# Top-k attention and a low-rank mixer: the top-k mask of the first two batches made by ScalarE and GpSimd

## The chip, the cores and the metric

The kernel runs on one core of a Trainium2 chip, in one launch. The metric is device time in microseconds. The core's engines are TensorE (PE; its weight loads are PEld), VectorE (DVE), ScalarE (ACT), GpSimd (POOL) and SyncE (SP, which only issues transfers here); each works through its own instructions in order and waits for the others by semaphores.

## What is computed

Top-k attention over 8 batches, 8 heads, 576 positions, 64 features per head, and then a token-mixing and MLP block over 512 channels:

```python
scores = scale * np.matmul(q, k.transpose(0, 1, 3, 2))      # 576 x 576 for each head
kth = np.partition(scores, -32, axis=-1)[..., -32:-31]      # the 32nd largest of each row
scores = np.where(scores >= kth, scores, -1000000000.0)
scores = scores - np.max(scores, axis=-1, keepdims=True)
attn = np.exp(scores)
attn = attn / (np.sum(attn, axis=-1, keepdims=True) + 1e-09)
x = np.matmul(attn, v)                                      # heads side by side: (B, S, 512)

h = x.transpose(0, 2, 1) @ U @ V                            # low-rank mixing of positions
u = x + h.transpose(0, 2, 1)
out = u + np.maximum(u @ w_ch1, 0.0) @ w_ch2
```

Of each row of scores only the 32 largest get a weight; the other 544 must come out as zero.

## The kernel before

The heads are taken in pairs, 4 pairs to a batch, 32 in all. A pair has five steps: four row tiles of 128 rows, with one chunk of 576 scores for each of the two heads, and a fifth step in which the last 64 rows of both heads share one chunk. So there are 160 steps; step n belongs to pair g and tile t by `g, t = divmod(n, 5)`. The work of a step is written as a generator, `front`, whose parts the main loop calls one by one to place them among the work of other steps. The program's order on each engine is the order of these calls.

VectorE finds the threshold: `max` gives the eight largest of a row, `match_replace` strikes them out, and four rounds of this give the 32nd largest in `ms[c][:, 7:8]`. Then the mask is made in one of two ways: on VectorE, after the Exp, by one instruction that compares, multiplies and sums; or, for the second chunk of a two-chunk step, on GpSimd ahead of the Exp, by adding -3e38 to every score below the threshold.

```python
    def weigh(chunk, E, nmax, total=None):
        nc.scalar.activation(E, chunk, AF.Exp, bias=nmax, scale=SCALE, accum_out=total)

    def front(g, t):
        # ... chunks: the scores; Es: the tiles for the weights; sums: columns of den ...
        for c in order:
            ms[c] = first[:, c]
            nc.vector.max(ms[c], curs[c])
        yield
        pooled = n == 2 and (g, t) != (NPAIR - 1, NT - 1)
        for i in range(1, TOPK // 8):
            if i == 1:
                nc.scalar.mul(nmax[:, 0:n], first[:, 0:n, 0], -SCALE)
                for c in range(1 if pooled else n):
                    weigh(chunks[c], Es[c], nmax[:, c : c + 1])
            for c in order:
                nxt = attn.tile([P, S], F32, tag="rr", name="rr", bufs=3)
                nc.vector.match_replace(nxt, ms[c], curs[c], NEG)
                curs[c] = nxt
            for c in order:
                ms[c] = small.tile([P, 8], F32, tag="m8", name="m8", bufs=8)
                nc.vector.max(ms[c], curs[c])
            yield
        if pooled:
            nc.gpsimd.tensor_scalar(Es[1], chunks[1], ms[1][:, 7:8], NEG, ALU.is_lt, ALU.mult)
            nc.gpsimd.tensor_tensor(chunks[1], chunks[1], Es[1], ALU.add)
        for c in range(1 if pooled else n):
            nc.vector.scalar_tensor_tensor(out=Es[c], in0=chunks[c], scalar=ms[c][:, 7:8],
                in1=Es[c], op0=ALU.is_ge, op1=ALU.mult, accum_out=sums[c])
        yield
        if pooled:
            weigh(chunks[1], Es[1], nmax[:, 1:2], sums[1])
        yield
```

`scores` multiplies q and k into PSUM and has ScalarE copy the result to SBUF (`Ssb`). `turns` transposes the weights on TensorE and copies them back with ScalarE (`PT`), in three parts. `values` multiplies them with v into `O`, which ScalarE copies to `XT`. At the end of a pair VectorE makes the reciprocal of the sums, after it has added 1e-9:

```python
    def inverse(g, lo, hi):
        den = dens[g][:, lo:hi]
        nc.vector.tensor_scalar_add(den, den, 1e-9)
        nc.vector.reciprocal(den, den)
```

The MLP of a batch is `mlp`, a generator of single matmuls on TensorE. `fill` lets so many of them run at each place of the loop that the MLP of one batch is spread over the attention of the next. In the first batch there is no MLP to run yet. The weights come as 64-bit numbers; `next_params` has them turned into 32-bit ones by ScalarE, VectorE (a shift) and GpSimd (two additions), during the first six pairs or so. The loop for the first batch:

```python
        if n < ALONE:                       # ALONE = 20: the first batch
            next(turning, None)             # transposes of step n-2, the last two parts
            next(turning, None)
            scores(*divmod(n + 1, CH))      # scores of the next step
            fill()
            if n >= 1:
                turning = turns(*divmod(n - 1, CH))
            if n >= 2:
                values(*divmod(n - 2, CH))
            next(here)                      # first round of step n
            next_params(1)
            next(turning, None)             # transposes of step n-1, the first part
            fill()
            next(last, None)                # the Exp of step n-1 that comes after GpSimd's mask
            next(ready, None)
            next(here)                      # second round
            # ...
            next(here)                      # third round
            # ...
            next(here)                      # the masks
            fill()
            continue
```

Of the kernel before, what the change touches and what calls it, by code (L numbers as in the profile page):

```python
# [8 lines left out]
F32 = mybir.dt.float32  # L9
U8 = mybir.dt.uint8  # L10
U32 = mybir.dt.uint32
AF = mybir.ActivationFunctionType
ALU = mybir.AluOpType

TOPK = 32
NEG = -3.0e38


RESCALE = 2.0**-112

TINY = 0.4 * 2.0**-15

# [2 lines left out]
def kernel(  # L25
# [28 lines left out]
    nc = tc.nc  # L54
    B, H, S, D = q.shape
    P = 128
# [4 lines left out]
    NT, TAIL = 4, 64  # L61
# [3 lines left out]
    NPAIR = H // 2  # L65
# [7 lines left out]
    const = ctx.enter_context(tc.tile_pool(name="const", bufs=1))  # L73
    loads = ctx.enter_context(tc.tile_pool(name="loads", bufs=1))
    attn = ctx.enter_context(tc.tile_pool(name="attn", bufs=2))
    small = ctx.enter_context(tc.tile_pool(name="small", bufs=8))
# [34 lines left out]

    nudge = const.tile([P, 1], F32, name="nudge")
    nc.vector.memset(nudge, TINY)

    def rows(t):
        return P if t < NT else TAIL
# [148 lines left out]
    def scores(g, t):  # L265


        qkT = qkTs[g]
        n = rows(t)
        S2 = attn.tile([P, 2 * (S + TAIL)], F32, tag="Ssb", name="Ssb", bufs=3)  # L270
        scs = [ps_s.tile([P, 2, 512], F32, tag="sc", name="sc") for _ in range(2)]
        for i, sc in enumerate(scs):
            for h in range(2):
                nc.tensor.matmul(  # L274
                    sc[slice(0, n) if t < NT else half(h), h, 0:HALF],
                    lhsT=qkT[half(h), 0, cols(t)],
                    rhs=qkT[half(h), 1, i * HALF : (i + 1) * HALF],
                    start=True,
                    stop=True,
                )  # L280
        if t == NT:
            for i, sc in enumerate(scs):
                for h in range(2):
                    nc.scalar.copy(
                        S2[half(h), i * HALF : (i + 1) * HALF], sc[half(h), h, 0:HALF]
                    )
            S2s[g, t] = [S2[:, 0:S]]
            return

        main = S2.rearrange("p (h n) -> p h n", h=2)  # L290
        last = S2[:, MAIN : MAIN + 2 * TAIL].rearrange("p (h n) -> p h n", h=2)
        copy = nc.vector.tensor_copy if g + t == 0 else nc.scalar.copy
        copy(main[:, :, 0:HALF], scs[0][:, :, 0:HALF])  # L293
        nc.scalar.copy(main[:, :, HALF:MAIN], scs[1][:, :, 0 : MAIN - HALF])
        nc.scalar.copy(last, scs[1][:, :, MAIN - HALF : HALF])  # L295
        S2s[g, t] = [S2[:, 0:S], S2[:, S : 2 * S]]

    def weigh(chunk, E, nmax, total=None):

        nc.scalar.activation(E, chunk, AF.Exp, bias=nmax, scale=SCALE, accum_out=total)  # L300

    def front(g, t):

        if t == 0:
            dens[g] = small.tile([P, 2 * NT + 1], F32, tag="den", name="den", bufs=3)
        chunks, den = S2s.pop((g, t)), dens[g]
        n = len(chunks)
        E2 = attn.tile([P, 2 * S], F32, tag="E", name="E", bufs=3)  # L310
        Es = [E2[:, c * S : (c + 1) * S] for c in range(n)]
        sums = [den[:, 2 * t + c : 2 * t + c + 1] for c in range(n)]
        probs[g, t] = E2
        curs, ms = list(chunks), [None] * n
        first = small.tile([P, 2, 8], F32, tag="first", name="first", bufs=3)
        nmax = small.tile([P, 2], F32, tag="nmax", name="nmax", bufs=4)
        order = (1, 0) if n == 2 else (0,)
        for c in order:
            ms[c] = first[:, c]
            nc.vector.max(ms[c], curs[c])  # L320
        yield
        pooled = n == 2 and (g, t) != (NPAIR - 1, NT - 1)
        for i in range(1, TOPK // 8):
            if i == 1:
                nc.scalar.mul(nmax[:, 0:n], first[:, 0:n, 0], -SCALE)
                for c in range(1 if pooled else n):
                    weigh(chunks[c], Es[c], nmax[:, c : c + 1])
            for c in order:
                nxt = attn.tile([P, S], F32, tag="rr", name="rr", bufs=3)
                nc.vector.match_replace(nxt, ms[c], curs[c], NEG)  # L330
                curs[c] = nxt
            for c in order:
                ms[c] = small.tile([P, 8], F32, tag="m8", name="m8", bufs=8)
                nc.vector.max(ms[c], curs[c])  # L334
            yield
        if pooled:
            nc.gpsimd.tensor_scalar(Es[1], chunks[1], ms[1][:, 7:8], NEG, ALU.is_lt, ALU.mult)  # L337
            nc.gpsimd.tensor_tensor(chunks[1], chunks[1], Es[1], ALU.add)  # L338
        for c in range(1 if pooled else n):
            nc.vector.scalar_tensor_tensor(  # L340
                out=Es[c],
                in0=chunks[c],
                scalar=ms[c][:, 7:8],
                in1=Es[c],
                op0=ALU.is_ge,
                op1=ALU.mult,
                accum_out=sums[c],
            )
        if t == NT:
            del qkTs[g]  # L350
        yield
        if pooled:
            weigh(chunks[1], Es[1], nmax[:, 1:2], sums[1])
        yield

    def turns(g, t):
# [18 lines left out]

    def inverse(g, lo, hi):
        den = dens[g][:, lo:hi]
        nc.vector.tensor_scalar_add(den, den, 1e-9)
        nc.vector.reciprocal(den, den)

    def values(g, t):
# [155 lines left out]
    CH = NT + 1  # L537
# [27 lines left out]
    t = 0  # L565
# [3 lines left out]
    turning = ready = iter(())  # L569
    fronts = {}  # L570
    for n in range(STEPS + 2):
        g, t = divmod(n, CH)
        if n < STEPS:
            if t == 0 and g + 1 < NP:
                load(g + 1)
            if t == 1 and g + 1 < NP:
                ready = prep(g + 1)
            fronts[n] = front(g, t)
            next(fronts[n])
        here, last = fronts.get(n, iter(())), fronts.pop(n - 1, iter(()))  # L580
        if n >= ALONE - 1 and n <= ALONE:

            list(turning)
            if n < ALONE:
                scores(*divmod(n + 1, CH))
            list(turns(*divmod(n - 1, CH)))
            if n < ALONE:
                values(*divmod(n - 2, CH))
                next(here)
            values(*divmod(n - 1, CH))  # L590
            if n < ALONE:
                inverse(g, 0, 2 * NT)
                next(here)
                mixing.append(mixed(g, 1))
                fill()
                next(here)
                next(here)
                continue
            fill()
            scores(*divmod(n + 1, CH))  # L600
            next(here)
            while mixing:
# [3 lines that stand above are left out]
            next(last, None)  # L606
            next(here)
            fill()
            next(here)
            next(here)  # L610
            fill()
            continue
        if n < ALONE:
            next(turning, None)
            next(turning, None)
            scores(*divmod(n + 1, CH))
            fill()
            if n >= 1:
                turning = turns(*divmod(n - 1, CH))
            if n >= 2:  # L620
                values(*divmod(n - 2, CH))
            next(here)
            next_params(1)
            next(turning, None)
            fill()
            next(last, None)
            next(ready, None)
            next(here)
            fill()
            if n >= 2 and (n - 2) % CH == NT:  # L630
                mixing.append(mixed((n - 2) // CH, 3))
            next(here)
            if t == 1:
                next_params(1)
            next(here)
            fill()
            continue
        fill()
        next(turning, None)
        fill()  # L640
        next(turning, None)
        fill()
        next(ready, None)
        fill()
        if n - 2 >= ALONE:
            values(*divmod(n - 2, CH))
        if n + 1 < STEPS:
            scores(*divmod(n + 1, CH))
        next(here, None)
        next_params(1)  # L650
        if n - 2 >= ALONE and (n - 2) % CH == NT:
            mixing.append(mixed((n - 2) // CH, 4))
        fill()
        next(here, None)
        fill()
        if n <= STEPS:
            turning = turns(*divmod(n - 1, CH))
        next(turning, None)
        fill()
        next(here, None)  # L660
        next(last, None)
        if t in (1, 3):
            next_params(1)
        next(here, None)
        fill()
# [33 lines left out]
```

## Time and profile before

| | |
|---|---|
| median of 3 runs | 1859.95 us (1859.87 to 1863.38) |
| span of the profiled run | 1861.6 us |
| TensorE busy | 1750.6 us (94%) |
| VectorE busy | 1617.2 us (87%) |
| ScalarE busy | 1008.1 us (54%) |
| GpSimd busy | 635.7 us (34%) |
| mean granted TensorE clock | 0.966 |

The page also cuts the span into 40 slices and gives each a digit, the busy share in tenths:

```profile
PE   4565789999999999999999999999999999999999
DVE  7999999999999999999999999999999999996000
ACT  4666677555655555555555555555555555554111
POOL 4556466433333332323233332332323332322000
PEclk7677799999999999999999999999999999999999
```

Each digit stands for 46.5 us. TensorE's row and its clock are lower for the first five slices, which are the first batch; VectorE is nearly full from the second slice to the last batch, and then has nothing to do while TensorE runs the last MLP. An average over the whole span says little about a change that touches two batches of eight, so the times are read by stages below. In the groups of the trace a row has the line, the engine and the operation, the tiles written and read with their shapes, the count, the busy time in microseconds, the mean of one in nanoseconds, and behind the second bar the idle time just before, with what ended it.

### The profile page before, as it was taken

The numbers are of one execution on the slowest core, as the hardware profiler recorded it, in microseconds if no ns is written. First come the engines' busy times: TensorE is split into PE (matmuls) and PEld (weight loads), VectorE is DVE, ScalarE is ACT, GpSimd is POOL, SyncE is SP. The second block draws the span as 40 slices with busy tenths as digits, with TensorE's granted clock in tenths as the row PEclk, the third lists the DMA queues.
The fourth block names the chain that finished last, engine by engine and source line by source line (L and its number), as shares of the span: only waits on it lengthen the run. The fifth ranks groups of instructions, "written<-read, shape, count | busy, mean of one in ns | idle before, by whom it ended". The sixth has DMA issues, their size and how long they took to land.

```text
span 1861.6 us, 29241 instructions
## 1 busy us (share of the span) xinstructions
PE 1750.6 (94%) x10528; PEld 1324.0 (71%) x10528; DVE 1617.2 (87%) x3316; ACT 1008.1 (54%) x2466; POOL 635.7 (34%) x432
## 2 busy tenths in 40 slices
PE   4565789999999999999999999999999999999999
PEld 3443556787777877788777877788777877788677
DVE  7999999999999999999999999999999999996000
ACT  4666677555655555555555555555555555554111
POOL 4556466433333332323233332332323332322000
PEclk7677799999999999999999999999999999999999
DMA  3222222101000010110001010101001010000000
GB/s 98 76 72 75 63 81 81 28 23 32 15 21 22 23 29 21 30 25 24 23 13 31 21 32 20 28 22 27 14 24 27 25 30 21 10 8 7 6 14 12
DMA packets 127296, 58.23 MB, mean 31 GB/s; under 512 B 89904, under 2 KB 124976, under 8 KB 127152
## 3 DMA queue, kind: packets, MB, share of 16 engines
q1 hardware_dynamic: 126096, 56.10, 11.3%
q8 instruction: 84, 1.38, 0.3%
q14 instruction: 60, 0.49, 0.1%
q10 hardware_dynamic: 1056, 0.26, 0.1%
HBM read 46.89 MB, written 9.44 MB: 30 GB/s over the span
## 4 chain that ended last, share of the span: by engine, by line
PE 84%; DVE 10%; ACT 4%; issue 1%; POOL 1%; DMA 0%; POOLq 0%; SPq 0%; DVEq 0%; ACTq 0%
PE mm L472 27%; PE mm L491 26%; PE sc L274 9%; PE O L403 6%; PE tp L367 6%; DVE rr L330 4%; DVE m L334 3%; PE O L390 2%; PE up L447 2%; PE O L400 1%; DVE first L320 1%; PE tp L254 1%; PE tp L519 1%; PE up L449 1%; PE tp L372 1%
## 5 line engine op out<-in xcount | busy, mean ns | idle before, releaser
L334 DVE MAX8 m<-rr 128x8 f32<-128x576 f32 x864 | 614.8, 749 | 5.5
L491 PE MATMUL mm<-hT,w 128*128 128x256 f32 (+1 forms) x2048 | 562.2, 410 | 0.0
L472 PE MATMUL mm<-uT,w 128*128 128x256 f32 (+1 forms) x2048 | 557.9, 411 | 1.5 <-ACT hT L484 1.5
L337 POOL TENSOR_SCALAR E<-Ssb,m 128x576 f32<-128x576 f32 x127 | 285.2, 2246 | 650.7 <-DVE m L334 512.7
L472 PEld LDWEIGHTS mm<-uT,w 128*128 128x128 f32 x2048 | 363.3, 190 | 108.6 <-issue 27.6
L491 PEld LDWEIGHTS mm<-hT,w 128*128 128x128 f32 x2048 | 360.5, 190 | 97.7 <-issue 22.5
L330 DVE MATCH_REPLACE8 rr<-m,rr 128x576 f32<-128x576 f32 x576 | 427.8, 743 | 0.0
L367 PE MATMUL tp<-ident,E 128*128 128x128 f32 x1152 | 184.7, 285 | 53.8 <-ACT E L300 38.7
L368 ACT COPY PT<-tp 128x512 f32<-128x512 f32 x288 | 168.4, 585 | 114.9 <-PE tp L367 113.0
L300 ACT ACTIVATE E<-Ssb,nmax 128x576 f32<-128x576 f32 x288 | 223.8, 778 | 5.9 <-POOL Ssb L338 0.7
L367 PEld LDWEIGHTS tp<-ident,E 128*128 128x128 f32 x1152 | 144.9, 147 | 106.9 <-ACT E L300 50.7
L274 PE MATMUL sc<-qkT 64*128 64x288 f32 (+1 forms) x1280 | 212.5, 454 | 0.3 <-ACT Ssb L293 0.3
L330 DVE MATCH_REPLACE8 rr<-first,Ssb 128x576 f32<-128x576 f32 x288 | 211.8, 742 | 0.0
L320 DVE MAX8 first<-Ssb 128x8 f32<-128x576 f32 x288 | 205.4, 750 | 0.9 <-ACT Ssb L295 0.9
L340 DVE SCALAR_TENSOR_TENSOR E<-Ssb,m,E 128x576 f32<-128x576 f32 x161 | 137.8, 856 | 65.6 <-ACT E L300 48.2
L338 POOL TENSOR_TENSOR Ssb<-Ssb,E 128x576 f32<-128x576 f32 x127 | 178.9, 1408 | 10.6
L484 ACT ACTIVATE hT<-mm 128x320 f32<-128x320 f32 (+1 forms) x256 | 104.4, 408 | 119.8 <-PE mm L472 119.0
L412 ACT COPY XT<-O 128x128 f32<-128x128 f32 x128 | 34.0, 266 | 215.1 <-PE O L403 215.1
L403 PE MATMUL O<-PT,va 128*64 128x128 f32 x2048 | 147.7, 289 | 0.0
L274 PEld LDWEIGHTS sc<-qkT 64*128 64x128 f32 (+1 forms) x1280 | 110.2, 187 | 51.7 <-issue 25.4
L504 DVE TENSOR_TENSOR oT<-uT,mm 128x320 f32<-128x320 f32 (+1 forms) x8 | 3.6, 455 | 146.6 <-PE mm L491 146.6
L403 PEld LDWEIGHTS O<-PT,va 128*64 128x64 f32 x2048 | 116.0, 143 | 16.8 <-issue 2.9
(73 smaller groups left out, 1484.3 us busy)
## 6 DMA issues: line engine op xcount, KB each, us to landing
raw<-in_moe_w_ch_dram SPq DMA_DIRECT2D x32, 512.0 KB, 3.7
va<-in_v_dram SPq DMA_DIRECT2D x64, 128.0 KB, 2.5
out_dram<-ob SPq DMA_DIRECT2D x64, 128.0 KB, 1.9
ld_q<-in_q_dram SPq DMA_DIRECT2D x63, 128.0 KB, 2.8
ld_k<-in_k_dram SPq DMA_DIRECT2D x63, 128.0 KB, 2.8
ld_ends<-in_q_dram SPq DMA_DIRECT2D x32, 32.0 KB, 2.2
ld_ends<-in_k_dram SPq DMA_DIRECT2D x32, 32.0 KB, 2.2
vd<-in_v_dram SPq DMA_DIRECT2D x64, 16.0 KB, 2.0
```

Source lines behind the costliest of these rows:

```text
L274: nc.tensor.matmul(sc[slice(0, n) if t < NT else half(h), h, 0:HALF], lhsT=qkT[half(h), 0, cols(t)], rhs=qkT[half(h), 1, i * HALF : (i + 1 ...
L300: nc.scalar.activation(E, chunk, AF.Exp, bias=nmax, scale=SCALE, accum_out=total)
L320: nc.vector.max(ms[c], curs[c])
L330: nc.vector.match_replace(nxt, ms[c], curs[c], NEG)
L334: nc.vector.max(ms[c], curs[c])
L337: nc.gpsimd.tensor_scalar(Es[1], chunks[1], ms[1][:, 7:8], NEG, ALU.is_lt, ALU.mult)
L338: nc.gpsimd.tensor_tensor(chunks[1], chunks[1], Es[1], ALU.add)
L367: nc.tensor.transpose(tp[:, j, :], E2[:, a : a + P], ident)
L368: nc.scalar.copy(PT[:, NT * h : NT * h + NT], tp)
L403: nc.tensor.matmul(O[half(h)], lhsT=va[:, h, j, :], rhs=PT[:, NT * h + j], start=False, stop=(j == NT - 1),)
L472: nc.tensor.matmul(ph[:, 0:w], lhsT=w1[:, cc, f * P : (f + 1) * P], rhs=uT[:, cc, lo:hi], start=(cc == 0), stop=(cc == NC - 1),)
L491: nc.tensor.matmul(po[:, 0:w], lhsT=w2[:, f, c * P : (c + 1) * P], rhs=hTs[f][:, 0:w], start=(f == 0), stop=(f == NF - 1),)
```

## The change

It makes the mask in another way in the first two batches, to take work off VectorE. For all steps of the first eight pairs but the last two steps of the first batch ("eased" steps), both chunks go ahead of the Exp through ScalarE and GpSimd. ScalarE computes `Relu((threshold - score) * 2^96)`: zero for a score at or above the threshold, and a huge number, at least the smallest gap that two numbers can have times 2^96, for any other. GpSimd subtracts it from the score. The Exp then gives zero for every score that was struck out, and its own running sum is the denominator. VectorE keeps only the search for the threshold; the addition of 1e-9 goes to ScalarE. The two sections of the main loop are put in a new order to suit: the masks and Exps of a step are called during the next step, and all its transposes one step later.

```diff
+WIDEN = 2.0**96
...
+    eps = const.tile([P, 1], F32, name="eps")
+    nc.vector.memset(eps, 1e-9)
...
+    def eased(g, t):
+        return g < 2 * NPAIR and (g, t) not in ((NPAIR - 1, NT - 1), (NPAIR - 1, NT))
...
+        final = small.tile([P, 2, 8], F32, tag="final", name="final", bufs=4)
...
-        pooled = n == 2 and (g, t) != (NPAIR - 1, NT - 1)
-        for i in range(1, TOPK // 8):
+        ease = eased(g, t)
+        pooled = n == 2 and not ease and (g, t) != (NPAIR - 1, NT - 1)
+        early = range(0 if ease else 1 if pooled else n)
+        rounds = TOPK // 8
+        for i in range(1, rounds):
...
-                for c in range(1 if pooled else n):
+                for c in early:
                     weigh(chunks[c], Es[c], nmax[:, c : c + 1])
...
-                ms[c] = small.tile([P, 8], F32, tag="m8", name="m8", bufs=8)
+                ms[c] = final[:, c]
+                if i < rounds - 1:
+                    ms[c] = small.tile([P, 8], F32, tag="m8", name="m8", bufs=8)
...
-        for c in range(1 if pooled else n):
+        for c in early:
             nc.vector.scalar_tensor_tensor(
...
-        if pooled:
-            weigh(chunks[1], Es[1], nmax[:, 1:2], sums[1])
+        if ease:
+            least = small.tile([P, 2], F32, tag="least", name="least", bufs=3)
+            nc.scalar.mul(least[:, 0:n], final[:, 0:n, 7], WIDEN)
+            for c in order:
+                nc.scalar.activation(
+                    Es[c], chunks[c], AF.Relu, bias=least[:, c : c + 1], scale=-WIDEN
+                )
+                nc.gpsimd.tensor_tensor(chunks[c], chunks[c], Es[c], ALU.subtract)
+            yield
+        for c in order:
+            if c not in early:
+                weigh(chunks[c], Es[c], nmax[:, c : c + 1], sums[c])
+        if ease and t == NT:
+            nc.scalar.activation(den, den, AF.Identity, bias=eps)
         yield
...
-        nc.vector.tensor_scalar_add(den, den, 1e-9)
+        if not eased(g, NT):
+            nc.vector.tensor_scalar_add(den, den, 1e-9)
...
         if n < ALONE:
-            next(turning, None)
-            next(turning, None)
             scores(*divmod(n + 1, CH))
+            list(turning)
             fill()
-            if n >= 1:
-                turning = turns(*divmod(n - 1, CH))
             if n >= 2:
                 values(*divmod(n - 2, CH))
             next(here)
+            next(last, None)
             next_params(1)
-            next(turning, None)
             fill()
-            next(last, None)
             next(ready, None)
             next(here)
             fill()
+            next(last, None)
...
             next(here)
             fill()
+            if n >= 1:
+                turning = turns(*divmod(n - 1, CH))
             continue
         fill()
         next(turning, None)
+        if eased(*divmod(n - 2, CH)):
+            next(turning, None)
...
         next(here, None)
+        if eased(*divmod(n - 1, CH)):
+            next(last, None)
         next_params(1)
...
             turning = turns(*divmod(n - 1, CH))
-        next(turning, None)
+        if not eased(*divmod(n - 1, CH)):
+            next(turning, None)
```

## The prediction

> **What bounds the kernel now.** I read the stages first, because the change touches only the first two of eight batches. From the starts of the `first` rows on VectorE I took the stage borders: step 0 starts at 11.0 us, step 20 (the second batch) at 223.9, step 40 (the third) at 434.5; VectorE's last attention work ends at 1709. The busy time of each engine in these four stretches (columns: stretch, length, PE, PEld, DVE, ACT, POOL busy with counts, granted clock, DMA share, GB/s):
>
> ```profile
> 11.00:223.90 212.90, 129.57 (x747) 88.05 (x744) 206.49 (x431) 133.13 (x305) 111.99 (x80) 0.71 0.27 75
> 223.90:434.50 210.60, 201.37 (x1238) 148.76 (x1238) 204.99 (x425) 139.03 (x330) 106.46 (x70) 1.00 0.18 50
> 434.50:1709.00 1274.50, 1266.76 (x7871) 967.62 (x7870) 1200.57 (x2452) 710.80 (x1769) 411.84 (x263) 1.00 0.09 22
> 1709.00:1861.00 152.00, 147.24 (x660) 116.31 (x658) 3.64 (x8) 22.34 (x59) 3.21 (x4) 1.00 0.04 11
> ```
>
> The reader is to see three regimes. In the first batch VectorE is busy 97% and TensorE 61%: VectorE alone sets the pace. In the second, TensorE is at 96% and VectorE at 97%: two bounds within 4 us of each other. From the third on TensorE is at 99.4% and its work alone sets the end. So a microsecond gained before 434 us reaches the end whole, since what follows is a fixed sequence of TensorE work; but in the second batch only TensorE's idle time, 210.6 - 201.4 = 9.2 us, can be gained. Next the page's costliest groups, for the operations concerned:
>
> ```profile
> L334 DVE MAX8 m<-rr 128x8 f32<-128x576 f32 x864 | 614.8, 749 | 5.5
> ...
> L337 POOL TENSOR_SCALAR E<-Ssb,m 128x576 f32<-128x576 f32 x127 | 285.2, 2246 | 650.7 <-DVE m L334 512.7
> ...
> L300 ACT ACTIVATE E<-Ssb,nmax 128x576 f32<-128x576 f32 x288 | 223.8, 778 | 5.9 <-POOL Ssb L338 0.7
> ...
> L340 DVE SCALAR_TENSOR_TENSOR E<-Ssb,m,E 128x576 f32<-128x576 f32 x161 | 137.8, 856 | 65.6 <-ACT E L300 48.2
> L338 POOL TENSOR_TENSOR Ssb<-Ssb,E 128x576 f32<-128x576 f32 x127 | 178.9, 1408 | 10.6
> ```
>
> One mask costs VectorE 856 ns by its row; GpSimd does one in 2246 + 1408 ns. Last, VectorE's and GpSimd's rows around the denominator's addition (start, duration, engine, line):
>
> ```profile
> 73.02 1.41 DVE L320 MAX8 first<-Ssb 128x8 f32<-128x576 f32 x2
> ...
> 73.94 1.40 POOL L338 TENSOR_TENSOR Ssb<-Ssb,E 128x576 f32<-128x576 f32 x1
> 74.35 1.02 DVE L378 TENSOR_SCALAR den<-den 128x9 f32<-128x9 f32 x1
> 75.40 0.21 DVE L379 RECIPROCAL den<-den 128x9 f32<-128x9 f32 x1
> ```
>
> An addition on 9 columns takes 1.02 us. It ends at 75.37, when GpSimd's operation ends at 75.34; at 217.44 the same line, with GpSimd idle, took 0.15 us. It is a wait that the trace books as work.
>
> **What the Trainium skill says.** "Advanced Engine Details and Errata", VectorE Performance Modes, Mode Summary: VectorE's second memory port is shared with GpSimd, and instructions of the two-port mode and GpSimd's block each other. The pair above agrees (1.02 us against 0.15). "ScalarE: Activation LUTs", What ACT_TABLE_LOAD costs: an activation with a per-partition bias takes about 280 ns + 0.833 ns per column; by that a Relu on 576 columns is an estimated 760 ns. The trace's Exp of that form takes 778. The page's Table sets section says that relu comes in every set, so that no new table load is due; in this trace Exp, Relu, Sign and Copy run with one load in all. "TensorE: Matmul & The Clock Gate", What's actually happening, says that TensorE is granted half clock until it has been busy for some 3.4 us; the 0.71 of the first stretch agrees, and at 115.15 us, after 3.78 us idle, four transposes took 1.11 us, at 120.89 0.66.
>
> **The change part by part.** 38 of the first 40 steps change: 18 in the first batch (15 of two chunks, 3 of one), 20 in the second (16 and 4).
>
> *VectorE loses work.* One mask goes per step. From 114.18, where one starts, to 114.93, where the next operation starts, is 0.75 us; with 0.02 to 0.07 of gaps I take 0.77. The addition goes for seven pairs, at 1.05 with its gap. First batch: 18 x 0.77 + 3 x 1.05 = 17.0 us. Second: 20 x 0.77 + 4 x 1.05 = 19.6. Together 36.6 us, 1.97% of 1860: even if all of it reached the end, the 2% line would just be missed.
>
> *GpSimd loses a little.* It now takes 1.41 us for each chunk rather than 3.65 for one of two. First batch: 33 x 1.41 = 46.5 in place of 15 x 3.65 = 54.8. No bound. But a two-port operation of VectorE's, the weights' shift of 0.4 us, may now meet it at another time.
>
> *ScalarE gains work.* Each chunk gets a Relu. Neighbouring activations overlap (Exp at 121.42, next start 122.10), so 0.68 us net; each step gets a small scaling of the threshold (0.15 net) and one more accumulator read (0.1 net); a pair gets the small addition, 0.2. First batch: 33 x 0.68 + 18 x 0.25 + 3 x 0.2 = 27.5 us; second, with 36 chunks: 24.5 + 5 + 0.8 = 30.
>
> *Order moves.* A step's masks and Exp are now made during the next step, after VectorE's last maximum is long there, so that ScalarE shouldn't stall on it. The transposes of step n-2 all follow the scores of n+1, and the value products follow the transposes directly. No ring of tiles seems short: E, scores and denominators have three buffers, and the last reader of each is a step ahead of the next writer.
>
> *First batch in sum.* ScalarE: 133.1 + 27.5 = 160.6 us of work in what would be 213 - 17 = 196. Of its idle time before, some 80 us, the largest named waits are these (groups of ScalarE between 11 and 224 us, idle before and releaser at the end):
>
> ```profile
> L368 ACT COPY PT<-tp 128x512 f32<-128x512 f32 x35 | 20.2, 577 | 9.7 <-PE tp L367 9.6
> ...
> L412 ACT COPY XT<-O 128x128 f32<-128x128 f32 x16 | 4.2, 266 | 22.3 <-PE O L403 22.3
> L325 ACT ACTIVATE nmax<-first 128x2 f32<-128x2 f32 (+1 forms) x20 | 4.1, 206 | 11.6 <-DVE first L320 11.5
> ...
> L398 ACT ACTIVATE x<-O,den 64x64 f32<-64x64 f32 x6 | 1.9, 308 | 12.5 <-DVE den L379 12.5
> ```
>
> Waits on TensorE for transposes and value products, 32 us, cannot be hidden in the new order either: the products (0.79 + 1.61 us at half clock) start only after the last copy of the transposes, and ScalarE's next instruction in order is the copy of their result. With the mixing's 8 us that is 40. The waits on VectorE (12.5 + 11.6) shrink as ScalarE falls behind it. So ScalarE needs 160.6 + 40 to 52 = 201 to 213 us, against 196 on VectorE: the bound passes to ScalarE, and of 17 us some 0 to 12 stay. I take 8.
>
> *Second batch.* At most 9.2 us by TensorE. ScalarE goes from 139 to 169 of some 205, 82%; in its first half, with the weights still being converted, nearer 90%, and it evicts the hidden layer's PSUM there. I take 4.
>
> **Sum:** 1860 - 8 - 4 = 1848 us.
>
> **The rivals.** (a) *VectorE stays the bound in the first batch*: for it speaks the copying of scores a step ahead, so that ScalarE may lag; then 17 + about 7 = 24 us, 1836. (b) *ScalarE becomes the bound, fully*: its waits on TensorE add to the new work instead of shrinking, and the first batch takes as long as before or 5 us longer, with TensorE starved of evictions in the second: 1860 to 1868. For it speaks that the new order puts two round trips one after the other; against it that TensorE can now do the next scores early. (c) *Nothing carries over*: if the second batch's pace is TensorE's alone, the gain there is nil and only the first counts: 1850. The table (0.4% of idle TensorE after 434 us) speaks against a gain being given back later.
>
> **Range and chances.** The range runs from near (a) to a mild (b): 1833 to 1863. Over 2% faster needs 1822.8, below the ceiling of 1823.4: 0.02. Over 2% slower, 1897, needs a stall of 1 us or more in every changed step: 0.02. Within 2%: 0.96. Faster at all I hold for three in four.
>
> **What would show it.** The masks gone from VectorE's row: 161 to 123; 33 + 36 = 69 Relus near 760 ns; GpSimd's subtraction near 1408. Step 20 starting at about 216 rather than 223.9, and step 40 at about 422. ScalarE's busy share in the first batch near 78%, VectorE's falling from 97% to about 93%, idle before `first` and released by ScalarE's copies. In the third batch on the same pace, about 55 us for a pair. I'd be wrong if VectorE stayed at 97% in the first batch (rival a), if the subtraction or Relu took much longer side by side, if the denominator's reciprocal inherited the wait of 0.9 us, or if a new TensorE wait on E opened in the second batch.

## The result and the profile after

The changed kernel takes 1922.37 us, median of 4 runs (1921.31 to 1923.86), against 1859.91 for the one before: 1.0332 times as long, with a 95% interval of 1.0314 to 1.035. It lost 62 us where 12 were expected to be won.

First the same cut by stages as of the kernel before (stretch, length, PE, PEld, DVE, ACT, POOL busy, granted clock, DMA share, GB/s). The borders are again the starts of step 0, of step 20 (now 234.4) and of step 40 (now 485.8); at 527.5 step 43 starts, from which on the steps have their old lengths:

```profile
11.00:234.40 223.40, 141.13 (x749) 95.89 (x745) 198.41 (x392) 158.62 (x377) 101.66 (x83) 0.66 0.25 72
234.40:485.80 251.40, 211.41 (x1211) 152.63 (x1211) 190.98 (x382) 162.81 (x394) 90.99 (x70) 0.95 0.14 42
485.80:527.50 41.70, 36.22 (x221) 28.42 (x220) 32.91 (x68) 23.19 (x57) 18.70 (x13) 0.96 0.12 31
527.50:1768.00 1240.50, 1236.34 (x7682) 944.09 (x7681) 1166.85 (x2384) 695.05 (x1731) 399.52 (x255) 1.00 0.09 22
```

and of the kernel before the stretch that answers to the last one, from its step 43 on:

```profile
468.90:1709.00 1240.10, 1235.95 (x7679) 943.55 (x7678) 1167.49 (x2384) 695.07 (x1731) 400.14 (x256) 1.00 0.09 22
```

The first batch is 10.5 us longer (223.4 against 212.9), the second 40.8 us (251.4 against 210.6). No engine is full in the second batch any more: TensorE 84%, VectorE 76%, ScalarE 65%, GpSimd 36%. That is the picture of a chain of waits, not of an engine that has too much to do. From 527.5 us on nothing differs: 1240.5 us where the same steps took 1240.1.

The starts of single steps, from VectorE's rows, show where it happens (us):

| step | before | after | after - before |
|---|---|---|---|
| 10 (third pair) | 114.93 | 109.73 | -5.2 |
| 15 | 168.05 | 166.86 | -1.2 |
| 20 (second batch) | 223.94 | 234.43 | +10.5 |
| 30 | 331.84 | 360.04 | +28.2 |
| 40 (third batch) | 434.46 | 485.79 | +51.3 |
| 43 | 468.90 | 527.46 | +58.6 |

The gain is there at first: the first step of pair 1 (step 5) took 10.23 us where it had taken 11.21. It is lost again from the third pair on.

The page's groups that answer to those of before:

```profile
L376 POOL TENSOR_TENSOR Ssb<-Ssb,E 128x576 f32<-128x576 f32 x69 | 97.3, 1429 | 269.2 <-ACT E L373 205.0
...
L357 DVE SCALAR_TENSOR_TENSOR E<-Ssb,final,E 128x576 f32<-128x576 f32 x123 | 104.9, 854 | 69.7 <-ACT E L304 53.6
```

38 masks have left VectorE, as counted. GpSimd's 69 subtractions take 1429 ns each and wait 205 us for the Relus. And the waits between engines up to step 43 (who waited, for whom, us, times, longest):

```profile
PE tp L396 <- ACT E L304: 76.2, 31, 11.1
ACT XT L442 <- PE O L433: 60.9, 33, 3.3
...
DVE first L332 <- ACT Ssb L299: 40.4, 12, 5.6
DVE den L409 <- ACT den L382: 19.4, 7, 5.0
...
ACT E L304 <- POOL Ssb L376: 13.9, 21, 1.3
...
DVE w L175 <- ACT w L165: 13.0, 7, 3.7
```

VectorE waits for the copies of the scores; TensorE waits for the Exp; ScalarE waits for TensorE's products and for GpSimd. Everyone waits for the next in a ring. One turn of it, during VectorE's step 38 in the second batch (the products in it are those of step 36, the scores those of step 39), from the rows of ScalarE, GpSimd and TensorE (start, duration, engine, line, in brackets the idle time before and its end):

```profile
463.01 1.44 ACT L373 ACTIVATE E<-Ssb,least 128x576 f32<-128x576 f32 x2
463.92 2.78 POOL L376 TENSOR_TENSOR Ssb<-Ssb,E 128x576 f32<-128x576 f32 x2 [11.87 <-DVE first L332]
465.37 0.78 ACT L304 ACTIVATE E<-Ssb,nmax 128x576 f32<-128x576 f32 x1 [0.91 <-POOL Ssb L376]
466.74 0.77 ACT L304 ACTIVATE E<-Ssb,nmax 128x576 f32<-128x576 f32 x1 [0.50 <-POOL Ssb L376]
467.65 1.09 PE L396 MATMUL tp<-ident,E 128*128 128x128 f32 x8 [1.65 <-ACT E L304]
468.35 1.07 ACT L397 COPY PT<-tp 128x512 f32<-128x512 f32 x2 [0.74 <-PE tp L396]
469.76 0.27 ACT L402 COPY PT<-tp 128x128 f32<-128x128 f32 x1 [0.34 <-PE tp L401]
471.28 1.09 PE L433 MATMUL O<-PT,va 128*64 128x128 f32 x16
472.42 0.27 ACT L442 COPY XT<-O 128x128 f32<-128x128 f32 x1 [1.42 <-PE O L433]
472.31 1.19 PE L278 MATMUL sc<-qkT 64*64 64x288 f32 x8
473.11 1.61 ACT L288 COPY Ssb<-sc 64x288 f32<-64x288 f32 x4 [0.42 <-PE sc L278]
475.07 1.44 ACT L373 ACTIVATE E<-Ssb,least 128x576 f32<-128x576 f32 x2
```

Relu, GpSimd's two subtractions, the two Exps, the transposes and their copies, the value products and their copy, the scores and their copies, and then the next step's Relu: 475.07 - 463.01 = 12.06 us for a turn, and step 38 is 11.93 us long. Between 469 and 471 us TensorE also works off MLP matmuls that stand in its queue between the parts. VectorE's row for step 39 starts right at the end of the last copy, after 1.94 us idle; its `final` of step 38 had begun at 471.40. This turn does not run through VectorE at all.

### The profile page after: what moved, and what is told of

The parts are those of the page before. It is cut to its first block, busy times and chain, and to the rows that moved or that the text cites. A ratio compares the mean times of both kernels' runs of the same rounds, so it can differ in the third digit from the quotient of the medians.

```text
span 1919.6 us, 29161 instructions
## 1 busy us (share of the span) xinstructions
PE 1776.9 (93%) x10528; PEld 1339.7 (70%) x10528; DVE 1594.3 (83%) x3234; ACT 1064.5 (55%) x2618; POOL 615.8 (32%) x439
## 4 chain that ended last, share of the span: by engine, by line
PE 73%; issue 1%; POOL 1%; ACT 0%; POOLq 0%; DVE 0%; DVEq 0%; ACTq 0%
PE mm L502 23%; PE mm L521 23%; PE sc L278 7%; PE O L433 5%; PE tp L396 5%; PE O L420 1%; PE up L477 1%; PE O L430 1%; PE tp L258 1%; PE tp L549 1%; PE up L479 1%; PE tp L454 1%; PE pT L465 1%; PE tp L401 1%; POOL oT L537 0%
## 5 line engine op out<-in xcount | busy, mean ns | idle before, releaser
L502 PEld LDWEIGHTS mm<-uT,w 128*128 128x128 f32 x2048 | 367.1, 192 | 114.1 <-issue 29.5
L351 DVE MAX8 m<-rr 128x8 f32<-128x576 f32 x576 | 409.8, 748 | 2.2
L354 POOL TENSOR_SCALAR E<-Ssb,final 128x576 f32<-128x576 f32 x96 | 215.8, 2248 | 542.0 <-DVE final L351 417.6
L278 PE MATMUL sc<-qkT 64*128 64x288 f32 (+1 forms) x1280 | 212.9, 454 | 8.6 <-ACT qkT L266 8.6
L351 DVE MAX8 final<-rr 128x8 f32<-128x576 f32 x288 | 204.9, 748 | 2.7
L376 POOL TENSOR_TENSOR Ssb<-Ssb,E 128x576 f32<-128x576 f32 x69 | 97.3, 1429 | 269.2 <-ACT E L373 205.0
L357 DVE SCALAR_TENSOR_TENSOR E<-Ssb,final,E 128x576 f32<-128x576 f32 x123 | 104.9, 854 | 69.7 <-ACT E L304 53.6
L355 POOL TENSOR_TENSOR Ssb<-Ssb,E 128x576 f32<-128x576 f32 x96 | 135.4, 1410 | 8.0
```

Of the source, the lines that this page charges most:

```text
L278: nc.tensor.matmul(sc[slice(0, n) if t < NT else half(h), h, 0:HALF], lhsT=qkT[half(h), 0, cols(t)], rhs=qkT[half(h), 1, i * HALF : (i + 1 ...
L502: nc.tensor.matmul(ph[:, 0:w], lhsT=w1[:, cc, f * P : (f + 1) * P], rhs=uT[:, cc, lo:hi], start=(cc == 0), stop=(cc == NC - 1),)
```

## The experiments

My theory by then was the ring; its rivals were the plain sum of work on ScalarE, a harm of the new order alone, and VectorE's own new waits (for the denominator, and in its shifts of the weights, which take longer beside GpSimd's work). The kernel before, run beside each group of these, took 1860.05 to 1861.02 us; a bracket gives the ratio to it and its 95% interval. Gains below are against 1922.4 unless another kernel is named; the changed kernel wasn't run again beside them, so that they are good to about 1 us.

**The two batches, and the order, each alone.**

```diff
-        return g < 2 * NPAIR and (g, t) not in (...)
+        return g < NPAIR and (g, t) not in (...)       # first_only
+        return NPAIR <= g < 2 * NPAIR                  # second_only, with the old first loop
+        return False                                   # order_only: new first loop, old masks
```

> The new mask in the first batch alone (18 steps), with the first batch's loop in its new order; the second batch as before. In the changed kernel step 20 started 10.5 us later than before and step 43 58.6 us later. If the two batches lose independently (theory A: each batch has its own bound on ScalarE's queue), this runs at about 1860 + 10 = 1870 us. If the second batch's loss is a delay handed over from the first (theory B), it runs at about 1860 to 1863, with the second batch catching up on TensorE's idle time, or far above 1880.

> The new mask in the second batch alone (20 steps), the first batch in its old order and with its old masks. Theory A: about 1860 + 48 = 1908 us, with VectorE waiting for the copies of the scores, 30 us or more. Theory B: within 10 us of 1860.

> The first batch's new order of calls with the old masks everywhere. If the order does the first batch's harm (scores first, all transposes at once, value products right behind them, two round trips to TensorE in a row), step 20 starts at 230 us or later and the run takes 1866 to 1870 us. If ScalarE's added work and the chain ScalarE - GpSimd - ScalarE do it, the order alone costs nothing: 1857 to 1862 us.

Measured: 1874.71 us for the first batch alone (1.0076, 1.0059 to 1.0093), 1909.78 for the second alone (1.0263, 1.0247 to 1.0278), 1864.78 for the order alone (1.0024, 1.0015 to 1.0032). 13.7 + 48.8 = 62.5 us: the batches lose independently, and four fifths is the second's. The order alone costs 4 us, between what I had given for harm and for none; step 20 then starts at 226.6, 2.6 us later than in the kernel before, where in the changed kernel it starts 10.5 later, so the order is not the bulk of it.

**What in the chain is long.** The first run narrows GpSimd's subtraction to 64 of 576 columns, the second the Relu too. Both leave out the mask for the other columns.

```diff
+                thin = slice(0, 64)
-                nc.gpsimd.tensor_tensor(chunks[c], chunks[c], Es[c], ALU.subtract)
+                nc.gpsimd.tensor_tensor(chunks[c][:, thin], chunks[c][:, thin], Es[c][:, thin], ALU.subtract)
# both_narrow: the Relu on [:, thin] as well
```

> The changed kernel, but GpSimd takes off the gap on the first 64 of 576 columns alone (the mask of the others is left out); ScalarE's instructions and every wait keep their places. If GpSimd's round trip of 1.4 and 2.8 us, on which ScalarE's queue waits before the Exp, is what lengthens the steps, this gives back most of the 62 us: 1880 us or less. If ScalarE's own work is the cause (60 us of it more in the changed kernel's page), or TensorE's answers to it, it stays above 1905 us.

> The changed kernel with Relu and subtraction on the first 64 of 576 columns (the mask of the others is left out). Beside the run with the narrow subtraction alone (1897 us) it takes only ScalarE's time away: some 0.43 us for each of 69 Relus, 30 us in all. If ScalarE's added work is what is left of the loss, this comes to 1870 us or less. If what is left is the order of calls and the waits on TensorE, it stays above 1885 us.

Measured: 1897.39 us (1.0197, 1.0182 to 1.0213) and 1865.15 (1.0028, 1.0016 to 1.004). The subtraction fell from 1429 to 324 ns and gave back 25 us, between the two numbers expected; the Relu fell from 768 to 341 ns, 29.5 us of ScalarE's time in all, and that gave back another 32. So a microsecond of ScalarE's work is paid in full, and of GpSimd's 76 us less (69 x 1.105) a third comes back. Neither GpSimd's round trip nor ScalarE's added work covers the 62 us alone. Since the order of the instructions and what each waits for stayed the same, I read this as the length of the links that counts.

**Cutting the ring by order.** Three moves, with the work unchanged: scores ahead of the transposes in the second batch; Relus and subtractions called at the end of their own step, so that GpSimd works beside the next step's transposes; both. In the last of these, and in the kernel with all three moves below, the Exp of the second batch also comes earlier, right after the next step's first round.

```diff
+        ahead = eased(*divmod(n - 1, CH)) and n + 1 < STEPS      # scores_first, second batch
+        if ahead:
+            scores(*divmod(n + 1, CH))
...
-        if n + 1 < STEPS:
+        if n + 1 < STEPS and not ahead:
...
         next(here)                                               # the masks' place in step n
         fill()
+        if eased(g, t):                                          # relu_early
+            next(here)
...
-            next(last, None)                                     # its old place, in both batches
```

> The changed kernel, with the scores of step n+1 called at the start of step n in the second batch too, ahead of the transposes and value products of step n-2. VectorE waited 32 us in the changed second batch for the copies of the scores. If the position of the scores behind the transposes makes a ring (Exp, transposes, values, scores, Relu, Exp), the second batch gives back 20 us or more: 1900 us or less. If TensorE and ScalarE need their 13 us for a step whatever comes first, it stays within 8 us of 1922.

> The changed kernel, with the Relus and subtractions of step n called at the end of step n, ahead of the next step's transposes and value products, and the Exp where it was. ScalarE's work is the same; GpSimd's round trip now lies beside other work of ScalarE. If the round trip costs what the narrow subtraction gave back (25 us), this runs at 1890 to 1902 us. If the narrow subtraction gained by something else (memory or port contention), or if ScalarE now stalls on VectorE's last maximum, it stays at 1915 us or more.

> Both at once, and the Exp called after the first round in the second batch, two fills earlier than before. If round trip and ring are separate losses, this is the sum of both gains: 1870 to 1885 us. If both are one loss, it is no better than the better of the two by more than 5 us.

Measured: 1892.46 us (1.0171, 1.0156 to 1.0186), 1883.41 (1.0129, 1.0112 to 1.0146), 1877.71 (1.0093, 1.0078 to 1.0108). They give back 30, 39 and 45 us. The sum of the first two gains would be 69: where the scores' move had brought 30 us alone, it brought 6 on top of the early Relus, so for the most part the two cut the same ring. (1877.71 lies in the range that I had given for two separate losses, which was too wide to tell them apart.) The early Relu gained more than the subtraction's length accounts for (39 against 25), so it shortened more than GpSimd's link.

**VectorE's wait for the denominator.**

```diff
+            late = n >= 2 and (n - 2) % CH == NT
+            if late:                 # a pair's end: the round first, then the reciprocal
+                next(here)
             if n >= 2:
                 values(*divmod(n - 2, CH))
-            next(here)
+            if not late:
+                next(here)
# and likewise in the second batch
```

> The changed kernel with VectorE's reciprocal of the sums placed after the first round of the step instead of ahead of it, once for each pair of the first two batches. VectorE waited 18 us for ScalarE's small addition there. If that wait is a loss of its own, this gives back 10 to 18 us (1905 to 1912 us). If VectorE would have waited elsewhere anyway, it gives back under 5 us.

Measured: 1919.44 us (1.0313, 1.0297 to 1.0328), 3 us back. VectorE's wait of 19.4 us was hardly a loss of its own.

**The value products.** ScalarE's largest wait is for these (60.9 us). They are moved behind the Relus and the conversion of the weights; alone, with the early Relus, and with both other moves. In the second batch this puts them behind the next step's scores too.

```diff
             fill()
-            if n >= 2:
-                values(*divmod(n - 2, CH))
             next(here)
             next(last, None)
             next_params(1)
+            if n >= 2:
+                values(*divmod(n - 2, CH))
# and likewise for the changed steps of the second batch
```

> The changed kernel with only the value products moved behind the Relus and the conversion of the weights; Relus, Exps and scores stay where the change put them. In the run with all three moves this move was worth 28 us. If ScalarE's waits for those products are a loss of their own, it gives back 20 to 30 us here too (1892 to 1902 us). If the move pays only once the other two have shortened the chain, it gives back under 10 us (1912 us or more).

> Early Relus and late value products, the scores of the second batch and its Exp left where the change put them. If scores ahead of the transposes matter beside the two others, this is 5 us or more above the 1849 us of all three; if not, it is within 3 us of it.

> Early Relus, scores first, and the value products moved behind the first round and the conversion of the weights, so that ScalarE has work while TensorE makes the products (it waited 46 us for them in the run without this move, 1877.7 us), and VectorE's reciprocal comes after the round as well. If those waits are what is left, this comes to 1850 to 1862 us. If ScalarE's sum of work is what is left, to 1870 us or more.

Measured: 1875.05 us alone (1.0077, 1.0062 to 1.0092), 1857.44 with early Relus (0.9983, 0.9975 to 0.9992), 1849.20 with all three (0.9938, 0.9923 to 0.9952). The one move gives back 47 us, over half more than the 30 that I had expected at most: step 20 starts 18 us earlier than in the changed kernel, so that it helps in the first batch too, where the scores had been ahead all along. Its waits up to 470 us:

```profile
DVE first L332 <- ACT Ssb L299: 28.6, 11, 5.6
...
ACT XT L442 <- PE O L433: 1.7, 2, 1.4
```

ScalarE's wait for the products fell from 60.9 to 1.7 us (3.4 up to its step 43), since it now has Relus and conversions to do while TensorE multiplies, and the products no longer stand between one step's Exp and the next step's Relu. The early Relus bring another 18 us on top, and the scores with the earlier Exp 8 more. All three moves give a kernel that beats the kernel before by 0.6%:

```profile
11.16:212.00 200.84, 127.09 (x747) 87.65 (x745) 195.30 (x394) 158.56 (x376) 102.04 (x83) 0.75 0.28 80
212.00:456.20 244.20, 233.48 (x1427) 172.67 (x1427) 218.33 (x447) 180.40 (x448) 108.91 (x83) 0.99 0.17 48
```

(The second stretch here ends where step 43 starts.) In the first batch VectorE is at 97% again, and the batch takes 200.8 us, 12 less than before. ScalarE does the same 158.6 us of work as in the changed kernel's 223.4. So in the first batch it was never its capacity; and up to step 43 it does 339.0 us of work in 445.1, where the changed kernel took 516.5 us for 344.6. VectorE's shifts still take 694 ns in the mean in this kernel (427 before), so that they aren't what the moves took away.

**ScalarE's work by itself.** To the kernel before, with its own masks, one Relu for each chunk of the same 38 steps is added; nothing reads the results. Once on all columns, once on 64.

```diff
         yield
+        if g < 2 * NPAIR and (g, t) not in (...):
+            for c in order:
+                nc.scalar.activation(chunks[0], chunks[c], AF.Relu, bias=nmax[:, c : c + 1], scale=-1.0)
         if pooled:
```

> The kernel before with one more Relu of 576 columns on ScalarE for each chunk of the same 38 steps, 69 in all, just ahead of the late Exp; nothing reads the results (they go into scores that are no longer needed), and masks and order stay as before. It adds some 47 us to ScalarE's queue and nothing else. If ScalarE's capacity is the cause, this costs 25 us or more (1885 us). If the place of the work in a chain through GpSimd is, it costs under 8 us (1860 to 1868).

> The kernel before with the 69 unread Relus on 64 of 576 columns: a third or so of ScalarE's time of the full ones (some 0.25 us net for each in place of 0.68), with the same positions and waits. The full ones cost 29 us. If the time on ScalarE's queue is what costs, this costs about 0.25 / 0.68 of it, 8 to 13 us (1869 to 1874). If it is the position or the waits, about as much as the full ones, 20 us or more.

Measured: 1889.27 us (1.0151, 1.0134 to 1.0168) and 1866.66 (1.0035, 1.0022 to 1.0048). ScalarE's rows of these Relus, first on all columns, then on 64:

```profile
L354 ACT ACTIVATE Ssb<-Ssb,nmax 128x576 f32<-128x576 f32 x69 | 53.6, 777 | 1.7 <-POOL Ssb L338 0.7
```

```profile
L354 ACT ACTIVATE Ssb<-Ssb,nmax 128x64 f32<-128x64 f32 x69 | 24.1, 349 | 1.7 <-POOL Ssb L338 0.7
```

53.6 us of work cost 29, and 24.1 us cost 6: the last 29.5 us of work cost 23. Step 20 starts only 4.3 us late with the long ones, step 43 is 25.6 us late. The loss is not spread over the steps: from step 20 to 23, 30 to 34 and 35 to 38 not 0.1 us is lost, and 18.9 us are lost where one pair passes to the next (steps 23 to 25, 28 to 30, 34 to 35 and 38 to 40). VectorE's masks wait for ScalarE's Exp, mostly there (from 224 to 480 us, the run with the long Relus, and then the kernel before):

```profile
DVE E L340 <- ACT E L300: 19.8, 7, 5.3
```

```profile
DVE E L340 <- ACT E L300: 3.1, 2, 2.2
```

That is another wait than the changed kernel's, where VectorE waited for the copies of the scores. So the kernel before could not take this work for nothing either, although ScalarE was busy 66% in its second batch. This run had been meant to tell capacity from chain and doesn't by itself: by my text its 29 us speak for capacity. The reordered kernel decides it, where as much ScalarE work runs in less time.

**GpSimd making both masks, ScalarE none.** All three moves, but the old two GpSimd operations for each chunk in place of the Relu.

```diff
+        for c in order:
+            if ease or (pooled and c == 1):
+                nc.gpsimd.tensor_scalar(Es[c], chunks[c], ms[c][:, 7:8], NEG, ALU.is_lt, ALU.mult)
+                nc.gpsimd.tensor_tensor(chunks[c], chunks[c], Es[c], ALU.add)
-        # the Relus and subtractions
```

> The same, but GpSimd makes both masks alone in its old way (2.25 + 1.41 us for a chunk) right after VectorE's last maximum, and ScalarE has no Relu. GpSimd then needs 7.3 us of a step's 10.2 for masks. If ScalarE's Relus are what costs, this beats the run beside it by 10 us or more and is at or below 1860. If GpSimd's long operations hold up VectorE's shifts and the sums of GpSimd's own work exceed the step while the weights are converted, it is slower than the run beside it.

Measured: 1862.73 us (1.0009, 1.0003 to 1.0016), 13.5 us more than with the Relus in the same order. Step 20 starts at 218.1 in place of 212.0, and it loses again up to step 29. Up to there, where 14.3 us are lost, ScalarE's Exp waits 31.1 us for GpSimd's masks, and VectorE's shifts and masks take some 5 us longer. Handing the long masks to GpSimd alone is no way out; which of the two reasons counts was not told apart by a run, but by these rows VectorE's longer work is a third of it at most.

**The order without the mask.** The kernel before with its old masks, and the value products of the first two batches late; then with the scores ahead in the second batch too.

> The kernel before, old masks, with the value products of the first two batches moved behind the first round and the conversion of the weights. The new mask with all three moves ran at 1849 us. If the gain of 11 us is the mask's and the moves only clear its way, this is within 4 us of 1860. If the moves alone would have brought it, it is at 1852 us or less. VectorE is busy 97% of the first batch here, so I expect the first.

> The same with the scores of the next step ahead of the transposes in the second batch. As beside: 1857 to 1864 us if the gain is the mask's, 1852 us or less if it is the order's.

Measured: 1855.92 us (0.9974, 0.9964 to 0.9983) and 1851.65 (0.9949, 0.9934 to 0.9964). I had expected neither to gain. In the kernel before ScalarE's wait for the products was nearly as long as in the changed one, up to step 43:

```profile
ACT XT L412 <- PE O L403: 49.4, 33, 3.3
```

There moving the products is worth 4 us, and 47 in the changed kernel: how much time is waited doesn't say what the wait costs. Of the 11 us of the best kernel, 8.5 come with an order alone, and the new mask adds about 2.4 by the medians; the two intervals overlap, and the two kernels weren't run side by side, so that whether the mask gains anything in the end stays open. At step 40 the kernel with the mask leads, 416.4 to 424.9 us, but at step 43 only 456.2 to 457.8: its step 42 takes 15.8 us, with TensorE busy 92% of it. By step 43 TensorE has done the same 360.6 us of work in either kernel, which I take for the reason that the lead is lost.

## Why the prediction was wrong

**What bounds the kernel** held where it said that time lost or won before the third batch reaches the end whole: 58.6 us at step 43 and 58.0 at the end of the same two traces (62.5 between the medians). **The parts' durations** held: Relu 768 ns for an estimated 760, the subtraction 1429 for 1408, 38 masks fewer. ScalarE's work in the first batch came to 158.6 us for 160.6 expected.

**"The bound passes to ScalarE, and of 17 us some 0 to 12 stay. I take 8"** was wrong by its waits. I gave ScalarE 40 to 52 us of idle time; it was 223.4 - 158.6 = 64.8. The wait for the value products didn't stay at 22 us: it was 35.2 in that stretch. The batch lost 10.5 us, which is near what the rival of a fully bound ScalarE named (as long as before or 5 us longer).

**"Second batch. At most 9.2 us by TensorE ... I take 4"** is the step that failed: that batch lost 49 us when it was changed alone. I reasoned from busy shares: ScalarE would go from 139 to 169 us of 205, 82%, so it would have room. It did 162.8 us of work and had no room, because its work and TensorE's answers stood one behind the other: a turn of 12.06 us, where the batch before had 210.6 / 20 = 10.5 us for a step. I had looked at rings of tiles and found none short; the ring of order, in which each step's Relu stands behind the last step's value products and scores in ScalarE's and TensorE's queues, I didn't follow. My sentence that the new order "puts two round trips one after the other" was put down for the first batch and not carried into the second, where a third, through GpSimd, was added to it. The sign that I had named for it came: TensorE waited 24.6 us for E in the second batch, in 14 waits, where it had waited 4.9 in 5. To a loss of over 2%, with a stall of 1 us or more in every changed step, I had given a chance of 0.02; 62 / 38 = 1.6 us came.

**VectorE's saving** was smaller than 36.6 us: up to step 43 it was busy 422.3 us where it had been busy 444.6. Its 32 large shifts of the weights took 756 ns in place of 427, as they now meet GpSimd's two-input operations: 32 x 0.33 = 10.5 us that I named and didn't size. The wait for the denominator was not 0.9 us but up to 5, since ScalarE's small addition comes behind the late Exp; that moving it away gave back only 3 us fits a VectorE that no longer sets the pace. And even with all three moves the 36.6 us did not reach the end: 12.0 us were won by step 20, and from there to step 43 only 0.7 more, within the cap of 9.2 us that the prediction had set for the second batch by TensorE's work.

**What stays open** is how much of the loss came through TensorE's clock. Up to step 43 its matmuls took 388.8 us in the changed kernel, 361.8 in the kernel before and 360.6 in the best one, at mean granted clocks of 0.82, 0.86 and 0.88, for the same work. Longer matmuls lengthen each turn of the ring; no run changed the clock alone.

## What to carry to other kernels

An engine that is busy 65% can be without room, if its next instruction waits for the answer to its last one: before work is moved onto it, write down one turn of the loop through all engines in their queue order, and compare its length with the step, not the busy share with 100%. If work must go into such a loop, put it where the engine waits anyway: one move of the value products behind the Relus was worth 47 us here, with not one instruction taken away. And try a new order without the new work: here one brought 8.5 of 11 us by itself.

## What the runs showed of the hardware

VectorE's shift of 128x512 words took 427 ns in the mean before and 756 ns in the changed kernel. Put beside GpSimd's rows, the changed kernel's 36 shifts (three of them smaller) fall into two kinds: 13 that begin with GpSimd idle take 0.39 us in the mean, 23 that begin during an addition, subtraction or multiplication of two tensors there take 0.99. Of the 23, the 20 large ones of `w` all ended 0.28 to 0.29 us after GpSimd's operation did. In the kernel before, five shifts began during GpSimd's comparison of one tensor with a threshold, and they took 0.41; in all runs together 50 such shifts took 0.42 in the mean, against 0.92 for 235 that began during an operation on two tensors and 0.41 for 323 with GpSimd idle. So it is not every GpSimd operation that holds VectorE up. The trace books such waits as busy time, so that VectorE's busy row overstates its work. TensorE's granted clock in the first two batches fell from 0.71 and 1.00 to 0.66 and 0.95, and was 0.75 and 0.99 in the best kernel. In the second batch its idle time had grown from 9.2 to 40.0 us; in the first it was 83.3 us before and 82.3 after, so that the sum of the pauses alone does not tell the clock.
